# Loading two of 128 chunks with sixteen 8-row DMAs each, in a decode attention kernel on one core

## The chip, the core and the metric

The kernel runs on one core of a Trainium2 chip. The metric is the device time of one execution, in microseconds (us), lower is better. An engine's short name in the profile: PE is TensorE (matmuls; PEld its weight loads), DVE is VectorE, ACT is ScalarE, POOL is GpSimd, SP is SyncE, which here only issues DMAs. Besides these the core has 16 DMA engines, which move the data between the chip's main memory (HBM) and the on-chip memory of 128 partitions (rows).

## The reference

One query position per head attends to 65536 keys and values. There are 32 query heads and 8 key/value heads, so four query heads share one key/value head; the head size is 128. Everything is bf16 at the ends.

```python
B, Hq, Hkv, Sq, Sk, D = 1, 32, 8, 1, 65536, 128
...
k = jnp.repeat(k, rep, axis=1)
v = jnp.repeat(v, rep, axis=1)
scale = D ** -0.5
scores = jnp.einsum("bhqd,bhkd->bhqk", q, k) * scale
p = _softmax(scores, axis=-1)
return jnp.einsum("bhqk,bhkd->bhqd", p, v)
```

Keys and values are 128 MiB each: the kernel must read 268.4 MB and does little arithmetic on each byte.

## The kernel before

**Chunks.** The sequence of one key/value head is cut into 8 chunks of 8192 positions (`NCH = 8`). A chunk of keys or of values is 2 MiB: 128 partitions of 64 positions x 128 elements, that is one contiguous run of 16 KB in HBM for each partition. With 8 heads there are 64 chunks of keys and 64 of values.

**The order.** Lines 110 to 117 write one list, `items`, of all 128 chunks in the order in which they are loaded and used. Keys of head `h` come with the values of the head before it (a little later still by `VLAG`), since the softmax of a head needs all its scores. So in the middle of the list keys and values alternate; the first chunks are keys alone, the last ones values alone. Chunk 45 is a chunk of keys (head 3, its fourth), chunk 90 one of values (head 5, its first).

**Buffers and the queue.** `buf` holds `NB = 9` chunk buffers; chunk `n` goes into buffer `n % 9`, so chunks 45 and 90 both go into buffer 0. `load(n)` (lines 245 to 258) emits on SyncE a wait until chunk `n - 9` has been used up (`freed`), and then one DMA of 128 rows x 16 KB at line 256. Every DMA adds 16 to a semaphore when it is done; each buffer has its own, `rdy[b]`, and `uses[b]` counts how often the buffer was loaded, so that whoever uses the chunk waits for `16 * uses[b]`. The last chunk alone is loaded in four column pieces (`TAIL = 4`, line 253), each with a semaphore of its own, so that its matmuls can begin before all of it has landed. SyncE does nothing but these waits and issues, in the order of the list.

**A chunk of keys** (`keys`): TensorE transposes it in 64 blocks of 128 x 128, eight to a PSUM bank (line 206); VectorE or ScalarE copies a bank out to `ktb` (lines 214 and 211); TensorE multiplies it with the head's four queries (`scores`, line 191). ScalarE copies the finished scores to `scs` (line 150) and VectorE takes a maximum (line 154). After the last chunk of a head, `softmax` takes the maximum over the partitions and ScalarE does the exponentials into `pts` (line 174).

**A chunk of values** (`values`): 64 small matmuls against `pts`, all adding up in one PSUM bank for a head (line 233). After a head's last chunk VectorE scales the sum (line 240). After all heads the result is transposed, copied and stored (lines 271 to 274).

The functions that the change touches, with the line numbers of the profile:

## Time and profile before

| | |
|---|---|
| median of 3 runs | 653.86 us (653.73 to 654.03) |
| the profiled execution | 653.82 us |
| its span, from first to last instruction | 652.0 us |
| PE busy | 510.2 us (78%) |
| PEld busy | 501.8 us (77%) |
| DVE busy | 294.3 us (45%) |
| ACT busy | 198.5 us (30%) |
| mean granted TensorE clock | 0.826 |
| DMA packets | 19063, 270.09 MB |
| read from HBM | 268.44 MB, 412 GB/s over the span |
| loads of 2048 KB, issue to landing | 34.0 us (keys, 64 of them), 33.0 us (values, 63) |
| the last chunk's pieces of 512 KB | 35.5 us |

A row of the profile's slices gives, for each of 40 equal parts of the span, a busy share in tenths. A DMA appears in three places: as an instruction on SyncE's queue (SPq), which is short, since it only hands the work out; as packets of the DMA engines, each with a start and a duration; and as 16 increments of its semaphore when parts of it are done. "Issue to landing" is the time from the instruction to the last increment, time in the queue included. In the chain of waits, a line such as "DMA buf<-in_v_dram" is the time from that issue until the data had landed.

### The profile page before, as it was taken

To read this page: it belongs to the slowest core of one execution; us is meant where nothing else is said; L and a number is where in the kernel's file an instruction comes from. 1 tells how busy PE (TensorE), PEld (TensorE's weight loads), DVE (VectorE), ACT (ScalarE), POOL (GpSimd) and SP (SyncE) were. 2 spreads that over 40 slices of the span, in tenths; PEclk is the share of its full clock that TensorE was granted. 3 is DMA by queue.
4 is the path that set the end of the run, shared out by engine and by line. 5 is a ranking of instruction groups with operands and counts; after the bars stand their busy time and mean duration, and the time that the engine had idled before them with its cause. 6 is when DMAs were issued, how large, how long until landed. Compare 5 with 4: busy or idle time off the path is not lost.

```text
span 652.0 us, 25515 instructions
## 1 busy us (share of the span) xinstructions
PE 510.2 (78%) x12290; PEld 501.8 (77%) x12290; DVE 294.3 (45%) x475; ACT 198.5 (30%) x266; POOL 7.1 (1%) x22
## 2 busy tenths in 40 slices
PE   3988688879888689886888878787888768977553
PEld 3988688769888689886888778787888768977553
DVE  1866454445545355443445445444545334544300
ACT  1433522252222522225222252224322252222400
POOL 0000000000000000000000000000000000000000
PEclk9999686987868898877888778898787896787655
DMA  8999999999999999999999999999999999999983
GB/s 351 422 422 427 425 425 424 427 422 426 424 425 426 426 424 424 423 427 423 428 422 426 424 424 423 425 424 427 424 427 422 427 422 427 423 428 422 427 351 149
DMA packets 19063, 270.09 MB, mean 414 GB/s; under 512 B 2192, under 2 KB 2192, under 8 KB 2704
## 3 DMA queue, kind: packets, MB, share of 16 engines
q1 hardware_dynamic: 18960, 268.46, 97.3%
q8 instruction: 96, 1.57, 1.0%
q14 instruction: 7, 0.06, 0.0%
HBM read 268.44 MB, written 0.01 MB: 412 GB/s over the span
## 4 chain that ended last, share of the span: by engine, by line
PE 53%; DMA 30%; issue 8%; ACT 6%; DVE 2%; POOL 0%; SPq 0%; POOLq 0%
PE trb L206 33%; DMA buf<-in_k_dram 24%; PE qkb L191 10%; PE pvb L233 10%; DMA buf<-in_v_dram 6%; ACT pts L174 5%; DVE ktb L214 2%; ACT ktb L211 1%; DVE hpart L154 0%; POOL hmaxa L166 0%; SPq L253 0%; DVE hmax L162 0%; ACT negb L168 0%; PE qkb L271 0%; POOL identf L127 0%
## 5 line engine op out<-in xcount | busy, mean ns | idle before, releaser
L206 PE MATMUL trb<-ident,buf 128*128 128x128 bf16 x4096 | 374.5, 244 | 45.2 <-issue 33.2
L214 DVE COPY ktb<-trb 128x1024 bf16<-128x1024 bf16 x384 | 256.7, 691 | 252.5 <-PE trb L206 250.7
L206 PEld LDWEIGHTS trb<-ident,buf 128*128 128x128 bf16 x4096 | 280.8, 109 | 49.8 <-issue 37.1
L191 PE MATMUL qkb<-qT,ktb 128*128 128x4 bf16 x4096 | 182.9, 166 | 32.4 <-ACT ktb L211 32.4
L191 PEld LDWEIGHTS qkb<-qT,ktb 128*128 128x128 bf16 x4096 | 170.9, 101 | 33.7 <-ACT ktb L211 33.7
L211 ACT ACTIVATE ktb<-trb 128x1024 bf16<-128x1024 bf16 x128 | 131.3, 1026 | 162.8 <-PE trb L206 161.7
L233 PE MATMUL pvb<-pts,buf 128*128 128x4 bf16 x4096 | 117.0, 165 | 51.0 <-issue 30.6
L233 PEld LDWEIGHTS pvb<-pts,buf 128*128 128x128 bf16 x4096 | 111.2, 98 | 53.1 <-issue 37.7
L150 ACT ACTIVATE scs<-qkb 128x256 f32<-128x256 f32 x64 | 24.6, 384 | 237.3 <-PE qkb L191 237.3
L174 ACT ACTIVATE pts<-scs,negb 128x512 bf16<-128x512 f32 x32 | 40.8, 1426 | 0.3
L154 DVE TENSOR_REDUCE hpart<-scs 128x4 f32<-128x256 f32 x64 | 38.6, 603 | 1.8 <-ACT scs L150 1.8
L181 DVE RECIPROCAL recip<-lsum 128x4 f32<-128x4 f32 x8 | 1.4, 178 | 51.3 <-POOL lsum L179 51.3
L240 DVE TENSOR_TENSOR oT<-pvb,recip 128x4 f32<-128x4 f32 x8 | 1.3, 158 | 38.6 <-PE pvb L233 38.6
L166 POOL PARTITION_ALL_REDUCE hmaxa<-hmax x8 | 3.0, 374 | 559.0 <-DVE hmax L162 559.0
L131 PE MATMUL trb<-ident,qsb 32*128 32x32 bf16 x1 | 0.2, 179 | 10.9 <-DVE ident L130 10.9
L131 PEld LDWEIGHTS trb<-ident,qsb 32*128 32x128 bf16 x1 | 0.1, 100 | 10.9 <-issue 10.9
L174 ACT ACTIVATION_READ_ACCUMULATOR pts<-scs,negb 128x1 f32 x32 | 8.1, 253 | 0.0
L168 ACT ACTIVATE negb<-hmaxa 128x4 f32<-128x4 f32 x8 | 1.6, 206 | 11.1 <-POOL hmaxa L166 11.1
L130 DVE CAST ident<-identf 128x128 bf16<-128x128 f32 x1 | 0.2, 228 | 10.6 <-POOL identf L127 10.6
L179 POOL PARTITION_ALL_REDUCE lsum<-rsum x8 | 3.5, 432 | 43.8 <-ACT pts L174 43.8
L134 ACT ACTIVATE dscr<-identf 128x1 f32<-128x1 f32 x1 | 0.2, 203 | 8.6 <-POOL identf L127 8.6
L162 DVE TENSOR_REDUCE hmax<-hpart 128x4 f32<-128x32 f32 x8 | 1.7, 207 | 0.3
(11 smaller groups left out, 3.1 us busy)
## 6 DMA issues: line engine op xcount, KB each, us to landing
buf<-in_k_dram SPq DMA_DIRECT2D x64, 2048.0 KB, 34.0
buf<-in_v_dram SPq DMA_DIRECT2D x63, 2048.0 KB, 33.0
buf<-in_v_dram SPq DMA_DIRECT2D x4, 512.0 KB, 35.5
qsb<-in_q_dram SPq DMA_DIRECT2D x1, 8.0 KB, 1.7
out_dram<-orow SPq DMA_DIRECT2D x1, 8.0 KB, 1.4
```

The source lines that it names most:

```text
L150: t = emit("scalar", lambda e: e.activation(scs[s][:, cols], qkb[b][:, 0:T * R], AF.Copy), after=[tok] + scs_free[s], signal=True)
L154: t = emit("vector", lambda e: e.tensor_reduce(hp[:, h, c, :], scs[s][:, cols].rearrange("p (t g) -> p g t", g=R), AX.X, ALU.max), after=[ ...
L162: t = emit("vector", lambda e: e.tensor_reduce(hmax[:, hs], hp[:, h, :, :].rearrange("p c g -> p g c"), AX.X, ALU.max), after=[tok], signa ...
L166: t = emit("gpsimd", lambda e: e.partition_all_reduce(hmaxa[:, hs], hmax[:, hs], P, bass.bass_isa.ReduceOp.max), after=[t], signal=True)
L168: t = emit("scalar", lambda e: e.activation(negb[:, hs], hmaxa[:, hs], AF.Copy, scale=-scale), after=[t], signal=True)
L174: t = emit("scalar", lambda e, g=g, i=i: e.activation(pv[:, g, :], sv[:, g, :], AF.Exp, bias=negb[:, i:i + 1], scale=scale, accum_out=rsum ...
L179: t = emit("gpsimd", lambda e: e.partition_all_reduce(lsum[:, hs], rsum[:, hs], P, bass.bass_isa.ReduceOp.add), after=[t], signal=True)
L191: tk = emit("tensor", lambda e, t=t, off=off: e.matmul(qkb[b][:, t * R:(t + 1) * R], lhsT=ktb[:, off:off + P], rhs=qT[:, h * R:(h + 1) * R ...
L206: tk = emit("tensor", lambda e, t=t, i=i, bank=bank: e.transpose(trb[bank][:, i * P:(i + 1) * P], kv[:, t, :], ident[:, :]), after=[ready, ...
L211: t_ev = emit("scalar", lambda e, dst=dst, bank=bank: e.activation(ktb[:, dst], trb[bank][:, :], AF.Copy), after=[tk, kt_free[slot]], sign ...
L214: t_ev = emit("vector", lambda e, dst=dst, bank=bank: e.tensor_copy(ktb[:, dst], trb[bank][:, :]), after=[tk, kt_free[slot]], signal=True)
L233: tk = emit("tensor", lambda e, t=t, tau=tau: e.matmul(pvb[bank][:, 0:R], lhsT=vv[:, t, :], rhs=pts[s][:, tau * R:(tau + 1) * R], start=ta ...
```

## The change

Chunks 45 and 90 are no longer loaded by one DMA of 128 partitions, but by sixteen DMAs of eight partitions each, issued one after the other on the same queue and counted on the same semaphore. DMA `i` takes partitions `32 * (i // 4) + i % 4`, and every fourth one after it, up to eight: DMA 0 has partitions 0, 4, 8, ... 28, DMA 1 has 1, 5, ... 29, DMA 4 has 32, 36, ... 60, and DMA 15 has 99, 103, ... 127. The first eight DMAs cover partitions 0 to 63, the last eight 64 to 127. Each row is still 16 KB and contiguous in HBM. `uses[b]` rises by 16 for such a chunk, so its user waits until all sixteen DMAs are done. All other loads, their order, the buffers and the compute are as before.

```diff
@@ -18,6 +18,7 @@
 VLAG = 1
 VLAG_LAST = 0
 TAIL = 4
+NARROW = (45, 90)
 ACT_GROUPS = (3, 7)
@@ -253,8 +254,14 @@
                 emit("sync", lambda e, i=i: e.dma_start(
                     buf[b][:, i * w:(i + 1) * w], src[:, i * w:(i + 1) * w]), after=aft, dma=tail_sem[i])
             return [(s, 16) for s in tail_sem]
-        emit("sync", lambda e: e.dma_start(buf[b][:, :], src), after=aft, dma=rdy[b])
-        uses[b] += 1
+        if n in NARROW:
+            for i in range(P // 8):
+                rows = slice(32 * (i // 4) + i % 4, 32 * (i // 4) + 32, 4)
+                emit("sync", lambda e, rows=rows: e.dma_start(buf[b][rows, :], src[rows, :]), after=aft, dma=rdy[b])
+            uses[b] += P // 8
+        else:
+            emit("sync", lambda e: e.dma_start(buf[b][:, :], src), after=aft, dma=rdy[b])
+            uses[b] += 1
         return [(rdy[b], 16 * uses[b])]
```

## The prediction

> **What bounds the kernel now.** I read the page's slices and queue table first, then busy time by stretches, then the chain of waits, then SyncE's timeline. The page says that the transfers fill the span:

> ```profile
> DMA  8999999999999999999999999999999999999983
> q1 hardware_dynamic: 18960, 268.46, 97.3%
> q8 instruction: 96, 1.57, 1.0%
> ```

> The first line is the mean busy share of the 16 DMA engines in 40 slices. The 18960 packets split exactly: 127 loads x 128 rows + 4 pieces x 128 + 2 x 32 for queries and output + 133 DMAs x 16 end packets = 16256 + 512 + 64 + 2128. So a row of 16 KB is one packet, and every DMA so far closes on 16 engines, with 8 rows on each. Below them run 96 instruction packets of 16 KB.

> The stretches (PE, PEld, DVE, ACT, POOL busy, granted clock, DMA share, GB/s) show a steady rate and then a half-empty end:

> ```profile
> 200.00:300.00 100.00, 80.49 (x1963) 79.27 (x1959) 45.95 (x74) 33.88 (x47) 1.18 (x3) 0.86 1.01 425
> 400.00:500.00 100.00, 81.83 (x1960) 80.80 (x1960) 46.44 (x74) 29.47 (x39) 0.80 (x2) 0.83 1.01 425
> 600.00:629.00 29.00, 17.00 (x497) 16.59 (x493) 6.37 (x13) 9.14 (x14) 0.80 (x2) 0.66 1.00 423
> 629.00:636.00 7.00, 3.73 (x128) 3.57 (x128) 0.00 (x0) 0.00 (x0) 0.00 (x0) 0.50 0.61 254
> 636.00:646.00 10.00, 4.16 (x144) 3.99 (x144) 0.00 (x0) 0.00 (x0) 0.00 (x0) 0.50 0.50 206
> ```

> 425 GB/s over 16 engines is 26.6 GB/s each: 0.617 us for a row, 4.93 us for 8 rows, the pace of a load. From 636 to 646 us the share is 0.50: eight engines have nothing left, eight still run, at 206/8 = 25.8 GB/s each. Eight alone go no faster, so the limit lies with each engine or its own way into the memory, not with the sum.

> Which eight wait? Each load has 16 completion increments in the trace. For load 3 they span 1.94 us, for load 45 8.05 us (228.21 to 236.26), for load 90 14.71 us, for the last piece 19.26 us: there one group of eight ends at 629.4 to 635.0 us, the other at 646.6 to 648.6. The chains of back-to-back packets in the second group break at the instruction packets, 96/8 = 12 an engine, some 18/12 = 1.5 us lost at each. I call the groups light and heavy. The end hangs on the heavy ones:

> ```profile
> 612.70 35.94 DMA buf<-in_v_dram
> 648.63 0.05 issue
> 648.68 0.60 PE pvb L233 x16
> ```

> This is the chain of work: 612.70 + 35.94 = 648.64 us, the heavy eight's last rows, then 3.4 us of closing work to 652.0. TensorE, 78% busy, isn't the bound.

> **The change, part by part.** *Rows and engines.* Loads 45 (keys) and 90 (values) keep their 128 row packets, 2 MB each. But a DMA of eight rows has eight packets and reaches at most eight engines. If all sixteen use the same eight, each of these gets 16 rows in place of 8: +8 x 0.617 = 4.93 us a load, 9.87 us for both, and the other eight get 9.87 us less. No row of this trace shows which eight. The increments show only what each answer is worth: on the light eight the slack is 648.6 - 635.0 = 13.6 us at the slowest of them (629.4 at the fastest, 19.2); on the heavy eight there is none. I take the same eight every time, since nothing in the diff rotates them. For the light ones there is only a guess: instruction packets keep to eight engines, and whoever gave them these would rather take those that short DMAs don't fall on. I price it at 2 to 1 or a little better.

> [...]

> *The way into the memory.* Rows 0 to 63 (DMAs 0 to 7) and rows 64 to 127 (DMAs 8 to 15) go through the same eight engines now, while the other eight go on with the next load. In the old loads each engine had its own eight rows; now, for half of each narrow load, two engines may write where one wrote. The trace has no such pair, so I bound it. Without sharing: nothing more. With full, fair sharing: 8 rows at half rate on the eight narrow engines, another 4.93 us a load, and the other eight lose as much, which eats what they gained. I take the full sharing, by the nearest rows: the instruction packets take 1.0% x 16 x 652/96 = 1.09 us against 0.617 us for a row of the same size, so where two streams meet here, they pay in full; and eight engines alone made 25.8 GB/s each, so no engine has speed in reserve.

> [...]

> *End packets.* An engine now closes each row: 16 ends of about 9 ns instead of one, 15 x 9 = 0.14 us a load, 0.27 us in all. The nearest row for a pause between small DMAs is the last load's four 512 KB pieces, which land 1.24 to 1.26 us apart, at 419 GB/s: no pause shows.

> [...]

> *SyncE's queue.* Fifteen more issues a load:

> ```profile
> 205.92 0.33 SPq L256 DMA_DIRECT2D buf<-in_k_dram  x1
> 212.30 0.33 SPq L256 DMA_DIRECT2D buf<-in_v_dram  x1
> ...
> 426.80 0.33 SPq L256 DMA_DIRECT2D buf<-in_v_dram  x1
> 428.59 0.33 SPq L256 DMA_DIRECT2D buf<-in_k_dram  x1
> 434.37 0.33 SPq L256 DMA_DIRECT2D buf<-in_v_dram  x1
> ```

> Load 45: 205.92 + 16 x 0.33 = 211.2, before load 46 goes out at 212.30. Load 90: to 432.1, so load 91 is 3.5 us late, load 92 isn't. What hides it: the light engines reach a load some 22 us after its issue (228.21 - 205.92; 448.25 - 426.80). At the longest unblocked issue (0.737 us) the sixteen take 11.8 us, still hidden. If every one stalled as the worst of the tail did (4.247 us, ten loads outstanding), 68 us would overrun the 22 by 46; here five to seven loads are outstanding, so I count zero, and see no way to a gain. The wait of line 256 is the same, once per load; no wait is added, only a higher count for whoever reads buffer 0.

> **The sum**, against the profiled execution (653.82 us, span 652.0 and 1.8 around it; the median is 653.86). Light eight: 635.0 + 9.87 + 9.87 + 0.27 = 655.0 us for the slowest, 649.4 for the fastest. Heavy eight: 648.6 - 9.87 + 9.87 = 648.6. The end moves from 648.6 to 655.0, by 6.4: 653.8 + 6.4 = 660.2 us. This can be read as a share s of full sharing: 635.0 + 9.87 (1 + s) + 0.27 passes 648.6 at s = 0.35, so the gain ends there.

> **Rivals.**
> *Balance without sharing (faster).* The light eight take the rows at full rate: 645.2 us; the heavy end at 638.8. The end comes 3.4 us earlier: 650.4 us. For it: the empty half from 636 us. Against it: any sharing beyond s = 0.35, and one engine of the light group that is 5.6 us behind its first. It decides up to about s = 0.2.
> *The heavy eight get the rows (slower still).* The last landing is at 648.6 + 9.87 + 0.27 = 658.7 us without sharing, 10.1 us later, so 663.9 us; with sharing 20.0 us later, 673.8 us. For it: no row says which eight. Against it: only the guess above.
> *Sixteen engines after all.* If rows are cut, or successive DMAs rotate over the engines, each engine keeps its 2 x 8 rows' worth and only the 0.27 us is left: 654.1 us. Against: one packet a row, and each DMA starts anew.

> **How the numbers follow.** Forecast with sharing 0.42, heavy eight 0.25, balance without sharing 0.25, sixteen engines 0.08. What a measurement of this kernel can tell from no change is about 0.2%, 1.3 us. Faster by more than that: the balance alone, 0.25. Within it: sixteen engines, and 0.04 of the forecast where s is near 0.35, together 0.12. Slower: 0.38 + 0.25 = 0.63. The forecast's own range, s from 0.35 to 1, is 653.9 to 660.2, and I take its end. The range from 650 to 666 us reaches down to the balance's 650.4 and up past 663.9; it leaves out the heavy eight with sharing (673.8, 0.1) and the edges of the rest, 0.2 in all.

> **What would show it.** Right: loads 45 and 90 each with sixteen issues of 128 KB, increments from only eight engines each; after load 45 a stretch near 230 to 245 us below 425 GB/s while eight engines share; the last landing near 655 us, the busy share at the very end 0.50 or less on the other eight engines, and row packets longer than 0.617 us around the narrow loads. Balance instead: packets stay at 0.617 us, and the half-empty end shrinks from 17 us to under 7. Heavy: the half-empty end grows to 27 us or more. Sixteen engines: nothing in the stretches moves. I'm wrong in kind if the narrow issues stall SyncE for over 22 us, and a gap shows in the DMA share.

## The result, and the profile after

The changed kernel takes 685.60 us (median of 4 runs, 684.72 to 686.06), the kernel before 653.81 us beside it: ratio 1.0484, 95% interval 1.0466 to 1.0502, or 31.8 us slower. The prediction had the direction; its number, 660.2 us, and its range, up to 666, were far too low.

The profiled execution has a span of 684.3 us, against 652.0. First the page's slices (17.1 us each) and its queue table:

```profile
DMA  8999999999999999999999999999999999999961
GB/s 354 423 424 426 425 425 424 424 426 425 426 424 423 287 289 425 426 425 425 425 423 425 426 424 424 426 414 261 300 421 426 424 423 408 423 425 426 424 266 43
q1 hardware_dynamic: 19184, 268.46, 96.1%
```

Two dips stand out, in slices 14 and 15 (222 to 257 us) and 28 and 29 (462 to 496), and a longer tail at the end. In the dips the DMA engines still count as over 90% busy, though they move only about two thirds of the bytes (261 to 300 GB/s). So nothing ran dry; each byte took longer. The queue has 224 packets more: 2 loads x 16 DMAs x 8 ends is 256, less the 32 ends of the two DMAs replaced. So each DMA of eight rows used eight engines, and the rows weren't cut.

The same in stretches (PE, PEld, DVE, ACT, POOL busy, granted clock, DMA share, GB/s):

```profile
200.00:220.00 20.00, 16.37 (x414) 16.06 (x410) 11.15 (x19) 5.25 (x7) 0.04 (x1) 0.91 1.00 422
230.00:250.00 20.00, 14.48 (x284) 14.20 (x281) 7.88 (x12) 3.84 (x5) 0.00 (x0) 0.67 1.01 215
...
460.00:500.00 40.00, 18.41 (x461) 17.78 (x458) 9.73 (x18) 11.02 (x16) 0.80 (x2) 0.74 1.01 302
...
660.00:670.00 10.00, 3.74 (x128) 3.57 (x128) 0.00 (x0) 0.00 (x0) 0.00 (x0) 0.50 0.25 103
670.00:680.00 10.00, 5.06 (x172) 4.81 (x173) 0.00 (x0) 0.00 (x0) 0.00 (x0) 0.50 0.14 55
```

From 230 to 250 us the rate is 215 GB/s, half of the usual 425, at a DMA share of 1.01. In the trace's DMA records the row packets of all sixteen engines take about 1.25 us there (1.08 to 1.40), not 0.61. The slow time begins at 228.2 us, when the first engine has done its eight rows of partitions 0 to 63 and goes on to 64 to 127, and ends at about 250, when only the last engine's last rows are left (they land by 251.3). Before it, the first narrow rows, of partitions 0 to 63, still take 0.61 us. What the two stretches lost, against 425 GB/s, is 20 x (1 - 215/425) = 9.9 us and 40 x (1 - 302/425) = 11.6 us. With the 9.87 us of extra rows that is 31.4 us, of 31.8 measured.

The end is held by very few engines: a share of 0.14 is 2.2 of 16. The last piece's increments come at 653.3 to 653.4 us from two engines, at 658.9 to 663.6 from eleven, at 668.4 from one, at 680.5 and 680.9 from two. The chain of waits ends on those:

```profile
645.05 35.82 DMA buf<-in_v_dram
680.87 0.05 issue
680.92 0.60 PE pvb L234 x16
```

SyncE's timeline shows that the issuing wasn't the cause:

```profile
208.51 11.07 SPq L260 DMA_DIRECT2D buf<-in_k_dram  x16
219.62 0.44 SPq L263 DMA_DIRECT2D buf<-in_v_dram  x1
```

Sixteen issues take 11.07 us (10.64 for load 90), 0.69 each, and the engines are fully busy in that time (422 GB/s from 200 to 220 us).

### The profile page after: what moved, and what is told of

It is laid out like the page before. It is cut to its first block, busy times and chain, and to the rows that moved or that the text cites. A ratio compares the mean times of both kernels' runs of the same rounds, so it can differ in the third digit from the quotient of the medians.

```text
span 684.3 us, 25545 instructions
## 1 busy us (share of the span) xinstructions
PE 520.2 (76%) x12290; PEld 511.0 (75%) x12290; DVE 295.2 (43%) x475; ACT 198.4 (29%) x266; POOL 7.1 (1%) x22
## 3 DMA queue, kind: packets, MB, share of 16 engines
q1 hardware_dynamic: 19184, 268.46, 96.1%
q8 instruction: 96, 1.57, 0.9%
## 4 chain that ended last, share of the span: by engine, by line
PE 45%; DMA 37%; issue 8%; ACT 5%; DVE 2%; SPq 2%; POOL 0%; another core or an unknown queue 0%; POOLq 0%
DMA buf<-in_k_dram 31%; PE trb L207 28%; PE qkb L192 9%; PE pvb L234 8%; DMA buf<-in_v_dram 5%; ACT pts L175 4%; SPq L260 1%; DVE ktb L215 1%; ACT ktb L212 1%; DVE hpart L155 0%; SPq L254 0%; POOL hmaxa L167 0%; DVE hmax L163 0%; ACT negb L169 0%; PE qkb L278 0%
## 5 line engine op out<-in xcount | busy, mean ns | idle before, releaser
L207 PE MATMUL trb<-ident,buf 128*128 128x128 bf16 x4096 | 382.3, 247 | 59.1 <-issue 30.7
L207 PEld LDWEIGHTS trb<-ident,buf 128*128 128x128 bf16 x4096 | 286.8, 111 | 64.4 <-issue 34.6
L192 PEld LDWEIGHTS qkb<-qT,ktb 128*128 128x128 bf16 x4096 | 173.5, 102 | 35.8 <-ACT ktb L212 35.8
L234 PE MATMUL pvb<-pts,buf 128*128 128x4 bf16 x4096 | 117.1, 165 | 56.8 <-DMA buf<-in_v_dram 25.8
```

The lines of the kernel that those rows point to most:

```text
L192: tk = emit("tensor", lambda e, t=t, off=off: e.matmul(qkb[b][:, t * R:(t + 1) * R], lhsT=ktb[:, off:off + P], rhs=qT[:, h * R:(h + 1) * R ...
L207: tk = emit("tensor", lambda e, t=t, i=i, bank=bank: e.transpose(trb[bank][:, i * P:(i + 1) * P], kv[:, t, :], ident[:, :]), after=[ready, ...
L234: tk = emit("tensor", lambda e, t=t, tau=tau: e.matmul(pvb[bank][:, 0:R], lhsT=vv[:, t, :], rhs=pts[s][:, tau * R:(tau + 1) * R], start=ta ...
```

## The experiments

My theory at this point: what costs is not the number of DMAs but where the eight engines write. In a load of 128 rows, so the theory, each engine has eight rows of its own, its place, and I number the engines by these. The stages of loads alone, further down, show the places that they try. Rows 64 to 67 and 96 to 99 are one engine's (I call it the ninth), rows 92 to 95 and 124 to 127 another's (the sixteenth): with one engine writing into either from elsewhere, the sum is 406 and 405 GB/s, the loss of two engines at half rate. The first four engines have rows 0 to 3 and 32 to 35, rows 4 to 7 and 36 to 39, and so on: four-row DMAs that give each of them these rows run at 434 GB/s, and two-row DMAs that send two of them one place further at 404. No stage tries the other places one by one; I take them to follow on in the same way. DMAs 0 to 7 of the change then give the low eight engines their own rows, and DMAs 8 to 15 send them across, into the places of the other eight. Where the owner writes at the same time, I call that a meeting. The rivals: DMAs of eight rows are slow wherever they write; their number or their issue costs; or only the extra rows on the low eight count.

**One half of the narrow load or the other.** The first kernel keeps DMAs 0 to 7 (`range(8)`) of the two chunks and leaves rows 64 to 127 unread, the second keeps 8 to 15 and leaves rows 0 to 63 unread (the second's edit, against the changed kernel):

```diff
-            for i in range(P // 8):
+            for i in range(8, 16):
...
-            uses[b] += P // 8
+            uses[b] += 8
```

> Loads 45 and 90 bring only rows 0 to 63, by the first eight DMAs; rows 64 to 127 of these two are left out. The eight narrow engines move as many rows as before the change. Theory G and P: no packet over 0.62 us but beside instruction packets, 425 GB/s less the rows left out, and no loss: 652 to 655 us (the two heavy ones among the narrow eight still end the kernel). If 8-row DMAs are slow by themselves, half of the loss stays: near 669 us.

> Loads 45 and 90 bring only rows 64 to 127, by the last eight DMAs; rows 0 to 63 of these two are left out. Bytes, DMAs and rows an engine as with rows 0 to 63 alone. Theory G: packets of 1.25 us on all engines from the first of these rows to the last, 8 rows x 0.63 = 5 us a load at least and more where the narrow engines come to them at different times (8 us apart at load 45): 10 to 22 us over the kernel before, 664 to 676 us. Theory of slow 8-row DMAs: the same time as with rows 0 to 63.

Rows 0 to 63 alone: 653.38 us against 653.77, ratio 0.9995 (0.9985 to 1.0004). Rows 64 to 127 alone: 675.47 us, 1.0329 (1.0312 to 1.0347), 21.7 us slower, with no engine carrying a row more than before. The stretches behind load 45 and load 90, for rows 0 to 63 (the first line) and for rows 64 to 127:

```profile
222.00:246.00 24.00, 18.14 (x437) 17.85 (x435) 10.76 (x19) 11.02 (x16) 0.75 (x2) 0.79 1.01 425
```

```profile
222.00:246.00 24.00, 16.72 (x336) 16.18 (x335) 9.33 (x16) 6.61 (x10) 0.43 (x1) 0.57 1.01 228
454.00:486.00 32.00, 21.17 (x424) 20.30 (x421) 10.21 (x19) 11.04 (x16) 0.80 (x2) 0.68 1.01 266
```

Eight-row DMAs among the other loads run at 425 GB/s when each engine writes its own rows. Across, the loss is 24 x (1 - 228/425) + 32 x (1 - 266/425) = 23.1 us. The whole change less this half is 685.60 - 675.47 = 10.1 us, close to the 9.87 us of extra rows. So the two terms add up, and each has been seen by itself.

**The loads alone.** A kernel without any compute runs stages of loads one after another: narrow DMAs between two plain loads and four more, so that the other engines always have work. Its output is only the queries, so its time isn't compared. The third and fourth of the stages shown read what the other half of the rows would hold and so part the reading from the writing:

```python
among(lambda b: rows8(b, 0, 0)),      # written 0-63, read 0-63
among(lambda b: rows8(b, 64, 64)),    # written 64-127, read 64-127
among(lambda b: rows8(b, 64, 0)),     # written 64-127, read 0-63
among(lambda b: rows8(b, 0, 64)),     # written 0-63, read 64-127
among(lambda b: row1(b, 64)),         # one-row DMAs into rows 64-67, 96-99
```

> Loads alone, no attention: the output holds the queries, so the time is not that of the kernel. Twelve stages, each waited for: plain loads; 8-row DMAs of rows 0 to 63 alone, then of rows 64 to 127 alone; the same between plain loads (two before, four behind); the same with the rows of the source exchanged; one-row DMAs of rows 64-67 and 96-99, then of 0-3 and 32-35, between plain loads; 64-row DMAs of each half; plain loads again. Theory G (one engine that writes the partitions of the other eight halves all sixteen): row packets of 0.61 us in the plain stages, with rows 0 to 63 between plain loads, and of 1.25 us on all engines with rows 64 to 127, for one-row DMAs too, so total near 210 GB/s while they last. Theory P (only the two engines meeting in a partition share): one-row DMAs of rows 64 to 127 slow two engines of sixteen, the total stays above 370 GB/s. Theory R (what counts is which rows are read, not written): the stage that reads rows 64 to 127 and writes 0 to 63 is slow, and the one that reads 0 to 63 and writes 64 to 127 isn't; G and P expect the reverse.

Stretches of its busy stages, in the order of the code above, and then one of DMAs of 64 rows into partitions 0 to 63 (the columns after the busy POOL are the clock, the DMA share and GB/s):

```profile
84.00:94.00 10.00, 0.00 (x0) 1.00 1.02 436
120.00:131.00 11.00, 0.00 (x0) 1.00 1.02 210
172.00:182.00 10.00, 0.00 (x0) 1.00 1.01 208
226.00:236.00 10.00, 0.00 (x0) 1.00 0.99 424
262.00:276.00 14.00, 0.00 (x0) 1.00 1.01 404
344.00:358.00 14.00, 0.00 (x0) 1.00 1.01 206
```

Halving follows where the rows are written (210 and 208 GB/s), not where they are read (424). The fifth line was new: one-row DMAs use one engine, here writing into the place of one other engine. Only those two had packets of 1.22 us, and the sum fell by no more than what two at half speed lose (425 x 15/16 = 398; measured 404). That is the sharing I had counted on. So a single meeting of two engines is paid by the two. Eight meetings at once are paid by all sixteen, which pairs alone would explain, as eight pairs are sixteen engines.

Another stage shows that the meeting counts, and not the crossing. It has the eight-row DMAs of rows 64 to 127 with no other load beside them, so the owners of these rows have nothing to write:

```profile
52.00:61.00 9.00, 0.00 (x0) 1.00 0.49 189
```

Eight engines write across, half of the engines are busy, and the median row takes 0.61 us. Rows 0 to 63 alone give 184 GB/s.

**How many meetings it takes.** The same frame; only the number of engines that write across is changed, `k` rows a DMA:

```python
among(few(2, 64, 1), few(3, 64, 1)),          # rows 64..67, 96..99: one engine
among(few(2, 64, 1, 7), few(3, 64, 1, 7)),    # rows 92..95, 124..127: one engine
among(few(2, 64, 2), few(3, 64, 2)),          # two engines; then 4 and 8
```

> Loads alone again, the output holds the queries. Eight stages, each two plain loads, then DMAs of 1, 2, 4 or 8 rows of partitions 64 to 127 (16 such rows on each of the 1, 2, 4 or 8 lowest engines), then four plain loads: one row a DMA to the partitions that the ninth engine has in a plain load; one row a DMA to those that the sixteenth has; two, four and eight rows a DMA; then three stages of eight rows a DMA in which the engines come to them at different times, or behind rows 0 to 63 as in the change. Theory P (pairs): with n engines writing across, 2n of 16 have packets of 1.25 us, so the total is about 425 x (16 - n)/16: 398, 398, 372, 319 and 213 GB/s. Theory G (all): 213 GB/s as soon as a few write across, two already, since in the kernel all sixteen stayed at 1.25 us while only two still wrote across. One engine alone slowed one other before, so G then needs a count at which it begins.

One engine across (into the ninth's place, then into the sixteenth's), then two, four and eight:

```profile
18.00:32.00 14.00, 0.00 (x0) 1.00 1.01 406
69.00:83.00 14.00, 0.00 (x0) 1.00 1.01 405
119.00:133.00 14.00, 0.00 (x0) 1.00 1.00 207
172.00:185.00 13.00, 0.00 (x0) 1.00 1.02 208
222.00:233.00 11.00, 0.00 (x0) 1.00 0.96 197
```

Two suffice: all sixteen engines then have rows of 1.25 us, and two, four or eight make no difference to the rate. The slow time with two lasted 20 us, from 116 to 136, which is the 16 rows of each of the two engines at 1.25 us. Three more stages of this kernel have eight engines write eight rows each across. Where they come to these rows together, as in the change, the slow time lasts about 10 us (324 to 334); where two of them have eight rows of their own more and come late, 13 and 16 us (374 to 387, 270 to 286). So it goes on until the late ones are through.

**Where they meet.** Five stages tell a meeting apart from a mere foreign row:

```python
own = [0, 1, 2, 3, 32, 33, 34, 35]
among(steps(2, own, 4, 4), ...)                      # each engine its own rows
among(steps(2, [4 + r for r in own], 2, 4), ...)     # rows 4 and 8, ...: one engine further
among(steps(2, own, 2, 64), ...)                     # rows 0 and 64, ...: one of two across
among(steps(2, [64, 65, 96, 97], 2, 2), ...)         # rows 64 and 66: two in the ninth's place
among(steps(2, [64 + r for r in own], 2, 4), ...)    # rows 64 and 68: two across
```

> Loads alone, the output holds the queries. Five stages, each two plain loads, then short DMAs, then four plain loads: four rows a DMA, each engine in its own partitions; two rows a DMA, 4 and 8 and so on, so that the two lowest engines write partitions of the second and third lowest; two rows a DMA, 0 and 64 and so on (the second engine alone writes elsewhere, into the ninth's); two rows a DMA into one group of eight partitions (64-67, 96-99), so that three engines meet in one place; two rows a DMA, 64 and 68 and so on, as in the stage that was slow on all sixteen. If what counts is that two or more engines write any partitions but their own: 425, 213, 400, 213, 213 GB/s. If the two halves (0 to 63, 64 to 127) have to be crossed: the second stage stays near 400 or above. If each pair that meets counts, and one meeting is harmless for the rest: the fourth stage, one meeting of three engines, stays above 350 GB/s.

The first stage ran at 434 GB/s (18 to 24 us). Stages two to five:

```profile
62.00:74.00 12.00, 0.00 (x0) 1.00 1.01 404
110.00:122.00 12.00, 0.00 (x0) 1.00 1.01 404
160.00:178.00 18.00, 0.00 (x0) 1.00 1.00 302
214.00:230.00 16.00, 0.00 (x0) 1.00 1.01 213
```

The second and third stage have one meeting each (in the second, the first engine writes for the second, which itself writes for the third; the meeting that slows is of the second's writes with the third's own), and two slow engines. With three engines in one place those three take 2.0 us a row, and the other thirteen 0.76 us. Two separate meetings halve everything.

**The same two steps in the kernel.** Loads 45 and 90 read only rows 64 to 67 and 96 to 99, in one-row DMAs (one engine across), or these and the rows four further on, in two-row DMAs (two engines across):

```diff
-            for i in range(P // 8):
-                rows = slice(32 * (i // 4) + i % 4, 32 * (i // 4) + 32, 4)
+            for r in (64, 65, 66, 67, 96, 97, 98, 99):
+                rows = slice(r, r + 1)          # the other kernel: slice(r, r + 5, 4)
...
```

> Loads 45 and 90 bring only eight rows each, 64-67 and 96-99, one row a DMA, so one engine alone writes across; all other rows of these two loads are left out. By the stages of loads alone, one such engine slows one other: 425 GB/s nearly stays. The one engine has 8 rows at 1.25 us a load, 5 us more than before: up to 10 us over the kernel before if it is one of the heavy ones, none if it is light, so 650 to 664 us; all others have 9.9 us less to do. No stretch at 213 GB/s.

> As with one row a DMA, but two rows: 64 and 68, and so on, so that two engines write across; all rows but sixteen are left out of loads 45 and 90. By the stages of loads alone, all sixteen engines go at half rate while these two write: 8 x 1.25 = 10 us a load if they come together, 5 us lost on every engine, 10 us in all on those two and none on the others, which have 9.9 us less to do; stretches near 213 GB/s of 10 us or more at both loads. 653 to 670 us, over the run with one row a DMA if both are light, and the half-rate stretch is what tells the two apart.

One row: 645.78 us, 0.9878 (0.9863 to 0.9892), faster as so much is left unread. That is below the 650 to 664 us expected: the last landing is at 640.7 us and not at 648.6, as the engines that end the kernel have 9.9 us less to do, and the expectation had left this out of its lower end. Two rows: 654.02 us, 0.9996 (0.9986 to 1.0005). The stretch behind load 45, first with one engine across, then with two:

```profile
225.00:234.00 9.00, 9.00 (x225) 9.00 (x223) 4.75 (x8) 3.08 (x4) 0.00 (x0) 0.72 1.00 397
```

```profile
225.00:234.00 9.00, 9.00 (x205) 9.00 (x204) 5.80 (x11) 2.43 (x3) 0.00 (x0) 0.65 1.01 213
```

With 8 us more at 203 GB/s behind load 90, the second kernel ran 17 us at half rate, worth about 8.5 us. The two kernels differ by 8.2 us, for 16 rows of 16384. The threshold holds with the compute running.

**Sixteen DMAs that keep to their rows, and two that don't.** The first has sixteen DMAs of 128 rows x 1 KB, the second only two DMAs, of rows 0 to 63 and 64 to 127:

```diff
+            w = T * D // 16
+            for i in range(16):
+                emit("sync", lambda e, i=i: e.dma_start(
+                    buf[b][:, i * w:(i + 1) * w], src[:, i * w:(i + 1) * w]), after=aft, dma=rdy[b])
...
```

```diff
-            for i in range(P // 8):
-                rows = slice(32 * (i // 4) + i % 4, 32 * (i // 4) + 32, 4)
+            for rows in (slice(0, 64), slice(64, 128)):
...
```

> Loads 45 and 90 come by sixteen DMAs each, as in the change, but of 128 rows x 1 KB, so every engine writes only its own partitions. If the loss is in who writes where, nothing is lost but sixteen ends a load and the shorter packets: within 1 us of the kernel before. If it is in the count of DMAs or in SyncE's issues (10 to 11 us a load), 10 us or more stay.

> Loads 45 and 90 come by two DMAs each, rows 0 to 63 and rows 64 to 127. All sixteen engines are used alike, 8 rows each, but all at once in one half of the partitions, as in the stages of half loads (1.28 us a row, 205 to 213 GB/s). Sharing without any imbalance: 8 rows x 0.64 = 5.1 us a load more on every engine, about 10 us in all, 664 us; more, up to 670, if engines that come late keep the others slow. If only imbalance costs: 654 us.

Sixteen by columns: 655.19 us, 1.0022 (1.0013 to 1.0032), 1.4 us slower than 653.82. Two by halves: 677.88 us, 1.0368 (1.0352 to 1.0383), 24.1 us slower, though the load is spread over all sixteen engines (32 end packets a load): 64 rows give each engine four, and as eight engines have their places among them (eight-row DMAs of rows 0 to 63 ran at 436 GB/s with the loads alone), at least half of the rows lie in another's place. That is more than the 664 to 670 us expected. The stretches after loads 45 and 90:

```profile
222.00:246.00 24.00, 17.37 (x378) 17.09 (x379) 10.03 (x18) 6.28 (x9) 0.43 (x1) 0.68 1.01 241
452.00:488.00 36.00, 22.50 (x496) 21.95 (x494) 12.76 (x22) 12.42 (x18) 0.80 (x2) 0.74 1.01 269
```

They lose 24 x (1 - 241/425) + 36 x (1 - 269/425) = 23.6 us: the slow times last longer than the 10 us a load that eight rows at 1.28 us take. In the kernel by columns something else is seen, in SyncE's timeline:

```profile
207.39 23.28 SPq L260 DMA_DIRECT2D buf<-in_k_dram  x16
427.71 32.30 SPq L260 DMA_DIRECT2D buf<-in_v_dram  x16
```

Issuing took 23 and 32 us, the loads behind it came late, and the DMA share fell to 0.97 (220 to 240 us) and 0.86 (450 to 470). That is the SyncE mishap that the prediction feared, in a milder form and with another edit. Whether it made the 1.4 us isn't shown: the last landing moved by as much, from 648.6 to 650.0 us, but the packets are slower too. One of 1 KB takes 0.046 us, sixteen 0.74 against 0.61 for a row, and over eight rows an engine that is 1.0 us a load.

**One narrow load, and its place.** `NARROW = (45,)`, `(6,)` and `(118,)`:

> Load 45 alone is narrow. If each narrow load costs by itself (theory G: 16 rows at 1.25 us in place of 8 at 0.617 on the eight engines of low number, two of which are heavy, so 20.0 - 4.9 = 15.1 us and its ends), about 16 us over the kernel before, 670 us. If the 32 us come from the second load on a queue that the first has put out of step, well under 10 us.

> One narrow load, number 6 instead of 45, where the engines are 1.9 us apart and not 8. Theory G with a span (all engines lose half their rate from the first row written across to the last; an engine of the low eight needs 8 own rows and then 8 across): about 10 us for the rows across plus some 3 to 4 for the distance, half of that lost, 6.5 to 7, plus 4.9 for eight rows more: 11 to 12 us over the kernel before, 665.5 us. If the loss doesn't depend on the distance between the engines: 669 us, as for load 45 alone.

> One narrow load, number 118, where the engines are 18.9 us apart. Theory G with a span: 18.9 + 20 - 4.9 = 34 us at half rate, 17 lost, plus 4.9: 22 us over the kernel before, 675.7 us. If early and late engines miss each other there (the early ones are through before the late ones write across, so that fewer than two meet the rest), or if the distance doesn't count: 15 us or less, 664 to 669 us.

| narrow load | us | ratio (95%) | more |
|---|---|---|---|
| 45 | 669.10 | 1.0234 (1.0219 to 1.0249) | 15.3 us |
| 6 | 664.41 | 1.0163 (1.0148 to 1.0178) | 10.6 us |
| 118 | 669.66 | 1.0244 (1.0229 to 1.0259) | 15.9 us |

The stretches behind loads 6 and 45:

```profile
38.00:49.00 11.00, 6.85 (x144) 6.73 (x142) 5.07 (x9) 2.43 (x3) 0.00 (x0) 0.77 1.01 215
```

```profile
229.00:249.00 20.00, 13.57 (x280) 13.29 (x277) 7.33 (x12) 3.46 (x5) 0.00 (x0) 0.67 1.00 224
```

At load 6 the engines are still within 2 us of one another: the slow stretch loses 11 x (1 - 215/425) = 5.4 us, and 4.9 us of extra rows make 10.4. At load 45 they are 8 us apart, so some engine writes across for longer: 9.5 + 4.9 = 14.4. At load 118 I expected 675.7 us, and that missed; the expectation had named the reason as its other case. The stretches behind it:

```profile
587.00:599.00 12.00, 4.82 (x128) 4.61 (x125) 1.99 (x3) 1.82 (x2) 0.00 (x0) 0.78 1.00 212
600.00:610.00 10.00, 8.77 (x190) 8.59 (x188) 4.59 (x7) 2.43 (x3) 0.00 (x0) 0.76 0.99 401
612.00:620.00 8.00, 0.00 (x0) 0.00 (x0) 0.00 (x0) 0.00 (x0) 0.00 (x0) 0.50 0.96 203
```

By then the engines are so far apart that the early ones are done before the late two begin: two separate slow times, of 12 and 8 us, with a break between. 6.0 + 0.6 + 4.2 + 4.93 = 15.7 us. In these kernels a crossing costs about half of the time in which at least two engines write across.

## Why the prediction was right and wrong

- **What bounds the kernel: right.** The rate of the transfers sets the time: in the changed kernel the stretches below 425 GB/s and the extra rows make 31.4 of the 31.8 us.
- **Rows and engines: half right.** Eight engines a DMA, the same ones each time, 4.93 us a load: after less the crossing half gives 10.1 us for two loads, against 9.87. The packet count shows the eight engines (224 packets more), and rows 0 to 63 alone, at 425 GB/s behind load 45, show that they are the ones that have their places there. Wrong was the either/or of light or heavy eight. The landings of the last piece fit neither: six light and two heavy engines got the rows. With rows 0 to 63 alone this shows directly: two engines end at 646.7 and 648.0 us, as the heavy ones did before, and six at 638.1 to 638.5, 9.9 us earlier. Two heavy ones are enough to set the end. In the forecast light engines ended the kernel, at 655.0 us; in fact it is these two, at 680.9. So that the direction came out was in part luck.
- **The way into the memory: this step failed.** I called full, fair sharing by the two engines concerned the upper bound, 4.93 us a load, and took no row for a case with several pairs at once. One pair does share like that (two engines at 1.22 us, 404 GB/s in sum). From two separate pairs on (207 GB/s with two, 208 with four), all sixteen engines run at half rate, and not for eight rows but for as long as at least two engines write across. Measured by itself the term is 21.7 us for both loads, where the sum had 9.87 (s = 1). The share s was thus no number between 0 and 1. Where the engines are nearly in step the size was right: at load 6 the crossing cost 5.4 us, against 4.93 in the sum. What the sum left out is that at load 45 they come 8 us apart and at load 90 nearly 15, and that all sixteen are slow in between.
- **End packets and SyncE: small, as predicted.** The sixteen narrow issues took 11.07 and 10.64 us and stayed hidden, though the slack was less than the 22 us counted, which run to the first landing: an engine begins its eight rows 4.9 us before that; rows 0 to 63 in eight DMAs a load cost nothing that shows (653.38 us against 653.77).
- **Many DMAs in place of one: small, as predicted.** The prediction saw no pause between queued DMAs in the last load's pieces. Measured, sixteen by columns cost 1.4 us, and two by halves cost 24.1. Where they write decides, not how many they are.
- **The rivals and the range.** The nearest was the one I left out of the range, heavy engines with sharing at 673.8 us. Put in the measured 21.7 for its 9.87 and it gives 685.6. The landings agree: 648.6 + 9.87 + 21.7 = 680.2 us for a heavy engine with the rows, 680.5 to 680.9 measured. Balance without sharing didn't occur: with these rows half of each narrow load is written across, while the owners write the next load.

Open is why two meetings slow the engines that meet nobody (207 GB/s for all), while one meeting leaves them alone (406); three engines in one place slow them partly (0.76 us a row). The only meeting tried inside one half of the partitions was a single one, so whether two of these would do the same isn't known. No run points to a version that beats the kernel before: the one faster time left rows out.

## What to carry to other kernels

Split a load by columns, or keep 128 partitions whole: by columns no stretch at half rate was seen (372 and 330 GB/s behind the two loads), and sixteen DMAs for each of two loads cost 1.4 us in all, part of it perhaps the issuing, which didn't keep up. A DMA over part of the partitions can send engines into one another's rows. Among other loads, two such engines halved the core's transfers for as long as it lasted (207 GB/s, against 406 with one), so two DMAs of 64 rows cost more (24.1 us) than sixteen of 128 (1.4 us); with nothing else in flight, eight-row DMAs into the same rows lost nothing (189 GB/s from eight engines, 184 into their own rows). In a profile, look for a rate of one half at a DMA share of 1.0 (215 GB/s at 1.01, against 425): a queue running dry lowers the share as well (to 0.86 in the kernel by columns), and in these runs it was engines in each other's way.
